# Attention with a delta rule and two feed-forward layers: sixteen weight loads move from SyncE's queue to GpSimd's

## The chip, the core and the metric

The kernel runs on one core of a Trainium2 chip. TensorE (PE) multiplies matrices, VectorE (DVE), ScalarE (ACT) and GpSimd (POOL) compute elementwise, SyncE (SP) computes nothing and issues transfers; the transfers themselves run on 16 DMA engines. The metric is the device time of one execution in microseconds (us), as a median over runs.

## The reference, cut to what matters

```python
# q, k, v: (4, 8, 768, 48), beta: (4, 8, 768)
state = zeros((B, H, D, D))
for t in range(S):
    y[:, :, t] = einsum('bhd,bhde->bhe', q[:, :, t], state)
    v_old = einsum('bhde,bhd->bhe', state, kt)            # kt: normalized k
    state = state + bt * einsum('bhd,bhe->bhde', kt, vt - v_old)
x = y reshaped to (3072, 384)
h = x @ w_in;  g = softplus(h);  x = g @ w_out            # 384 -> 2048 -> 384
h = x @ w_in2; g = h * cos(h);   out = g @ w_out2         # 384 -> 2048 -> 384
```

## The kernel before

The sequence of 768 tokens is cut into 24 chunks of 32. For each group of four chunks the keys and queries are normalized, split into an fp16 high and low part and transposed (`norms`, `prep_k`, `prep_q`), multiplied with each other on TensorE (`gram`, line 606), and a small triangular system is solved on VectorE (`solve`). `step(n)` then carries the state over chunk n and leaves its result y16. A transposing DMA (line 786) writes y16 into `xt`, the input of the first feed-forward layer. Two chunks make a block of 256 tokens: `moe_block(0, j)` multiplies it with the first layer's weights (line 811 into the hidden layer, line 873 out of it). The second layer runs in blocks of 512 tokens after that.

The weights come from HBM as 64-bit floats, sixteen pieces f0 to f15 for each layer, 768 KB each. `conv` loads one piece and turns it into an fp16 high and low part: VectorE at lines 455, 457 and 459 assembles fp32 words in `cv`, ScalarE or VectorE at lines 470 or 474 writes the high part, VectorE at line 480 the low part. A piece lands in the buffer `raw` or in a weight buffer that is not needed yet (order lists print them as w_83, w_84, w_85 and w_86). So a load has to wait until line 459 of the piece before it in that buffer has read it. The transfers between the other stages go through small strips of 32 partitions (`bd_load`: bdKQ, bdA, bdT), four for each.

Nothing of the order is written by hand. `Plan.add` records each operation with its dependencies and the engines it may run on, and `Plan.greedy` simulates the engines and the DMA engines with built-in costs and so fixes, once, in which order each engine gets its instructions; many elementwise operations may go to two engines, and this choice is the planner's as well. On the chip each engine, and SP's and POOL's queue, runs its list strictly in that order: an instruction that waits holds up all behind it.

Of the kernel before, what the change touches and what calls it, by code (L numbers as in the profile page):

```python
# [56 lines left out]
class Plan:  # L57
# [59 lines left out]
    @staticmethod  # L117
    def after(o):

        return 0.65 + 0.9 + o["dma"] + o["slack"] if o["var"][0][0] == "SP" else 0.0  # L120

    def tails(self, succ):
        ops = self.ops
# [9 lines left out]
    def greedy(self, tail, succ, pred, back=None):  # L133
        ops = self.ops
        n = len(ops)
        engs = ("PE", "DVE", "ACT", "POOL", "SP", "-")
        free = {e: 0.0 for e in engs}
        soon = {e: [] for e in engs}
        now = {e: [] for e in engs}
        left = [len(p) for p in pred]  # L140
        ready = [[] for _ in range(n)]
        done = [False] * n
        dma_free = 0.0
        busy = {}
        var = [dict(o["var"]) if back is None else {back[i]: dict(o["var"])[back[i]]} for i, o in enumerate(ops)]

        def release(i):
            for e in var[i]:
                t = 0.0
                for f, end, raw in ready[i]:  # L150
                    t = max(t, end + (self.lat(f, e, raw) if back is None else self.lat(e, f, raw)))
                if back is not None:
                    t += self.after(ops[i])
                heapq.heappush(soon[e], (t, i))

        for i in range(n):
            if not left[i]:
                release(i)
        log = []
        port = {"DVE": 0.0, "POOL": 0.0}  # L160

        def held(e, i, st):

            if back is not None or e not in port or e == "DVE" and not ops[i]["port"]:
                return 0.0
            return max(0.0, port["POOL" if e == "DVE" else "DVE"] - st)

        while len(log) < n:
            best = None
            for e in engs:  # L170
                while soon[e] and (done[soon[e][0][1]] or soon[e][0][0] <= free[e]):
                    t, i = heapq.heappop(soon[e])
                    if not done[i]:
                        heapq.heappush(now[e], (-tail[i], i, t))
                while now[e] and done[now[e][0][1]]:
                    heapq.heappop(now[e])
                if now[e]:
                    st = free[e]
                elif soon[e]:
                    st = soon[e][0][0]  # L180
                else:
                    continue
                if best is None or st < best[0]:
                    best = (st, e)
            st, e = best
            free[e] = st
            while soon[e] and soon[e][0][0] <= st:
                t, i = heapq.heappop(soon[e])
                if not done[i]:
                    heapq.heappush(now[e], (-tail[i], i, t))  # L190
            item = heapq.heappop(now[e])
            i = item[1]
            c = var[i][e] + held(e, i, st)
            urgent = [a for a, b in soon[e] if a < st + c - self.SL and tail[b] > tail[i] + self.MARG and not done[b]]
            if urgent:
                room = min(urgent) - st + self.SL
                fit = [x for x in now[e] if not done[x[1]] and var[x[1]][e] <= room]
                heapq.heappush(now[e], item)
                if not fit:
                    free[e] = min(urgent)  # L200
                    continue
                item = min(fit)
                now[e].remove(item)
                heapq.heapify(now[e])
            i, t = item[1:]
            o, c = ops[i], var[i][e] + held(e, i, st)
            if len(var[i]) > 1:
                pn = self.PEN if st > self.EARLY else self.PEN0
                later = [max(free[e2], t) for e2, c2 in o["var"]
                         if e2 != e and max(free[e2], t) + c2 + pn[e2] < st + c + pn[e]]  # L210
                if later:
                    heapq.heappush(soon[e], (max(st, min(later)) + 1e-3, i))
                    continue
            if e == "SP" and back is None and dma_free > st + c + 0.65 + self.BACKLOG:
                heapq.heappush(soon[e], (dma_free - c - 0.65 - self.BACKLOG + 1e-3, i))
                continue
            done[i] = True
            if e == "PE" and back is None:
                c = self.pe_time(busy, st, c, o["cold"])
            end = st + c  # L220
            free[e] = end + o["hold"]
            if e == "POOL" or e == "DVE" and o["port"]:
                port[e] = end
            if e == "SP" and back is None:
                dma_free = max(end + 0.65, dma_free) + o["dma"]
                end = dma_free + 0.9 + o["slack"]
            log.append((st, end, e, i))
            for s, raw in succ[i]:
                ready[s].append((e, end, raw))
                left[s] -= 1  # L230
                if not left[s]:
                    release(s)
        return log
# [35 lines left out]
def dve(n, fast=False):  # L269
    return 0.068 + n / (1920.0 if fast else 960.0)  # L270
# [6 lines left out]
def pool(n):  # L277
    return 0.149 + n * 0.001883
# [7 lines left out]
def delta_moe_moe_kernel(ctx, tc, q, k, v, beta, mask, w1, w2, out):  # L286
    nc = tc.nc
    eng = {"PE": nc.tensor, "DVE": nc.vector, "ACT": nc.scalar, "POOL": nc.gpsimd, "SP": nc.sync}
# [38 lines left out]
    st = att.tile([P, 2, H, D], F32, name="st")  # L327
# [47 lines left out]
    def put(var, w, r, fn, **kw):  # L375
        return pl.add(var, w, r, fn, **kw)

    def dma(dst, src, w, r, eng_us, issue=0.56, **kw):
        put([("SP", issue)], w, r, lambda e: nc.sync.dma_start(out=dst, in_=src), dma=eng_us, **kw)  # L379

    def copy(out, in_, scale, w, r, n, ps=False, fast=True, only=None, **kw):
        var = [("ACT", act(n, ps)), ("DVE", dve(n, fast and not ps))]
# [38 lines left out]
    def wview(ph, f):  # L421
        return wbuf[ph][f // 2][:, f % 2].bitcast(F16).rearrange("p (o l n) -> p o l n", o=2, l=2)
# [17 lines left out]
    cvn = [0]  # L440

    def conv(ph, f, t, key):
        put([("SP", 0.475)], key, [("wp2",)] if ph else [],
            lambda e: nc.sync.dma_start(out=t(), in_=(w1, w2)[ph][f]), dma=2.18)
        c = cvn[0] % NCV
        cvn[0] += 1
        cv = cvb[c]
        cf = cv.bitcast(F32)
        n = 2 * DM
        ck = [("cv", c, 0), ("cv", c, 1)]  # L450

        def half(b):
            return t().bitcast(I32).rearrange("p o (n two) -> p o n two", two=2)[:, :, :, b]

        put([("DVE", dve(n, True))], ck, key, lambda e: nc.vector.tensor_scalar(
            cv, half(1), 0x07FFFFFF, 3, op0=ALU.bitwise_and, op1=ALU.logical_shift_left), port=True)
        put([("DVE", dve(n))], ck, key, lambda e: nc.vector.scalar_tensor_tensor(
            cv, in0=half(1), scalar=-0x40000000, in1=cv, op0=ALU.bitwise_and, op1=ALU.bitwise_or), port=True)
        put([("DVE", dve(n))], ck, key, lambda e: nc.vector.scalar_tensor_tensor(  # L459
            cv, in0=half(0), scalar=29, in1=cv, op0=ALU.logical_shift_right, op1=ALU.bitwise_or), port=True)  # L460
        if ph:
            copy(cf, cf, W_SC, ck, [], n)
        wk = [("w", ph, f, 0), ("w", ph, f, 1)]

        sc = 1.0 if ph else W_SC
        wv = lambda l: wview(ph, f)[:, :, l]

        def hi(e):
            if e == "ACT":
                nc.scalar.activation(out=wv(0), in_=cf, func=AF.Copy, scale=sc)  # L470
            elif ph:
                nc.vector.tensor_copy(out=wv(0), in_=cf)
            else:
                nc.vector.tensor_scalar_mul(wv(0), cf, sc)

        def lo(e):
            if ph:
                eng[e].tensor_tensor(out=wv(1), in0=cf, in1=wv(0), op=ALU.subtract)
            else:
                nc.vector.scalar_tensor_tensor(wv(1), in0=cf, scalar=sc, in1=wv(0), op0=ALU.mult, op1=ALU.subtract)  # L480

        put([("ACT", act(n)), ("DVE", dve(n, True))], wk, ck, hi, port=True)
        put([("POOL", pool(n)), ("DVE", dve(n))][0 if ph else 1:], wk, ck, lo, port=True)
# [92 lines left out]
    slack = [0.0]  # L576
# [363 lines left out]
    for n in range(4):  # L940
        prep_k(n)
        if n % 2:
            dst, keys = (bdKQ[:, :, 0:12], bdA22)[n // 2], [first[n - 1][1], first[n][1]]
            src = kg0[n // 2][:, :, 16 * C:].rearrange("p n (x t) -> p n x t", t=X2)
# [99 lines left out]
```

## Time and profile before

| | |
|---|---|
| median of 3 runs (lowest to highest) | 1028.8 us (1028.32 to 1029.23) |
| the profiled execution: its own time / its span | 1029.89 us / 1028.1 us |
| PE, DVE, ACT, POOL busy, share of the span | 91%, 65%, 65%, 34% |

The span runs from the first to the last instruction of the profiled execution; 1.8 us of its time lie around it. The page and the views below count in us from the span's start. SPq stands for SP's queue: the time in which it issues a transfer, waits included.

### The profile page before, as it was taken

How to read it: one execution, taken by the hardware profiler on the slowest of the kernel's cores; microseconds unless marked ns; L12 is line 12 of the kernel's file. 1: busy time of each engine (PE TensorE's matmuls, PEld its weight loads, DVE VectorE, ACT ScalarE, POOL GpSimd, SP SyncE). 2: the span in 40 equal slices, each digit the busy share in tenths (PEclk: the TensorE clock that was granted, in tenths of full speed). 3: DMA queues.
4: the chain of work that ended last, by engine and by line, in shares of the span. 5: the costliest groups of instructions: out<-in, count | busy, mean ns of one | idle time of the engine just before them, and what ended most of it. 6: DMA issues, size and time to landing. Idle time of an engine off the chain costs nothing.

```text
span 1028.1 us, 27541 instructions
## 1 busy us (share of the span) xinstructions
PE 933.6 (91%) x11552; PEld 681.6 (66%) x11552; DVE 669.6 (65%) x1199; ACT 665.2 (65%) x1256; POOL 353.4 (34%) x326
## 2 busy tenths in 40 slices
PE   2134899999999999999999999999999999999998
PEld 2124788889998899989998898644444444444443
DVE  9999887468648756964766665685555555455553
ACT  5344669677867877785767788866555555455554
POOL 3022236224523632362233344563332323323222
PEclk9555899999999999999999999999999999999999
DMA  7998796885776678476677842111001010100000
GB/s 202 275 253 213 165 242 155 184 193 129 178 180 134 142 175 181 103 149 162 134 178 204 207 101 78 47 62 62 1 9 54 1 61 1 31 32 1 31 1 32
DMA packets 317020, 121.85 MB, mean 119 GB/s; under 512 B 281440, under 2 KB 296928, under 8 KB 316896
## 3 DMA queue, kind: packets, MB, share of 16 engines
q1 hardware_dynamic: 316896, 120.09, 48.0%
q8 instruction: 91, 1.49, 0.6%
q14 instruction: 33, 0.27, 0.1%
HBM read 73.39 MB, written 37.22 MB: 108 GB/s over the span
## 4 chain that ended last, share of the span: by engine, by line
PE 69%; DVE 10%; ACT 6%; DMA 5%; SPq 5%; issue 3%; POOL 1%; ACTq 0%; DVEq 0%; POOLq 0%
PE psH L811 19%; PE accA L873 14%; PE accB L873 10%; PE psC L811 7%; PE psA L873 6%; PE psC L694 6%; SPq L379 5%; PE psY L811 4%; PE psY L694 2%; PE psA L606 2%; DMA qt<-q_dram 1%; DMA bdA<-kpd 1%; DVE st L404 1%; DVE cv L459 1%; ACT e L828 1%
## 5 line engine op out<-in xcount | busy, mean ns | idle before, releaser
L400 POOL TENSOR_TENSOR g<-g,g 128x512 f16<-128x512 f32 x191 | 228.2, 1195 | 495.3 <-ACT g L388 492.2
L811 PE MATMUL psH<-xt,w 128*128 128x256 f16 x1728 | 225.4, 273 | 1.5 <-DVE w L480 1.1
L388 ACT ACTIVATE g<-g 128x512 f16<-128x512 f32 x192 | 120.5, 628 | 106.5 <-DVE g L404 69.6
L873 PEld LDWEIGHTS <-w 128*128 128x128 f16 x1728 | 160.4, 97 | 18.5 <-issue 0.3
L811 PEld LDWEIGHTS <-w 128*128 128x128 f16 x1728 | 158.7, 98 | 19.8 <-DVE w L480 1.4
L873 PE MATMUL accA<-g,w 128*128 128x256 f16 x1152 | 154.7, 272 | 0.1
L873 PEld LDWEIGHTS <-v 128*128 128x128 f16 x864 | 84.6, 98 | 102.4 <-issue 0.5
L811 PEld LDWEIGHTS <-v 128*128 128x128 f16 x864 | 84.5, 98 | 100.4
L409 ACT ACTIVATE e<-e 128x512 f32<-128x512 f32 x96 | 60.4, 629 | 81.7 <-DVE e L404 81.6
L400 DVE TENSOR_TENSOR g<-psH,e 128x512 f32<-128x512 f32 x96 | 66.0, 688 | 59.8 <-ACT e L411 53.0
L873 PE MATMUL accB<-g,w 128*128 128x256 f16 x576 | 93.1, 272 | 0.0
L694 PEld LDWEIGHTS <-bdA 128*128 128x128 f16 x2256 | 74.1, 98 | 19.0 <-issue 16.7
L811 PE MATMUL psH<-xu,v 128*128 128x512 f16 x351 | 83.4, 379 | 0.0
L811 PE MATMUL psC<-xu,v 128*128 128x512 f16 x342 | 82.1, 379 | 0.0
L873 PE MATMUL accA<-g,v 128*128 128x512 f16 x288 | 78.0, 379 | 0.3 <-POOL g L400 0.3
L873 PE MATMUL accB<-g,v 128*128 128x512 f16 x288 | 77.8, 379 | 0.0
L873 PE MATMUL psA<-g,v 128*128 128x512 f16 x288 | 77.7, 379 | 0.0
L828 ACT ACTIVATE e<-psH 128x512 f32<-128x512 f32 x96 | 56.4, 588 | 28.2 <-PE psH L811 27.8
L694 PEld LDWEIGHTS <-bdKQ 128*128 128x128 f16 x1840 | 61.2, 98 | 16.6 <-issue 15.0
L694 PE MATMUL psC<-u,bdA 128*128 128x48 f16 x1680 | 58.9, 185 | 14.6 <-DMA bdA<-kpd 7.5
L411 ACT ACTIVATE e<-e,hpi 128x512 f32<-128x512 f32 x96 | 69.1, 721 | 2.9
L411 ACT ACTIVATE e<-e 128x512 f32<-128x512 f32 x96 | 59.9, 624 | 1.1
(145 smaller groups left out, 1438.0 us busy)
## 6 DMA issues: line engine op xcount, KB each, us to landing
kpd<-kp SPq DMA_DIRECT2D x24, 512.0 KB, 4.1
bdA<-kpd SPq DMA_DIRECT2D x96, 128.0 KB, 4.5
bdKQ<-kqd SPq DMA_DIRECT2D x92, 128.0 KB, 4.1
kqd<-kq SPq DMA_DIRECT2D x20, 512.0 KB, 5.5
raw<-w_dram SPq DMA_DIRECT2D x12, 768.0 KB, 5.6
w<-w_dram SPq DMA_DIRECT2D x10, 768.0 KB, 6.7
v<-w_dram SPq DMA_DIRECT2D x10, 768.0 KB, 6.1
qt<-q_dram SPq DMA_DIRECT2D x24, 256.0 KB, 4.2
```

Source lines behind the costliest of these rows:

```text
L379: put([("SP", issue)], w, r, lambda e: nc.sync.dma_start(out=dst, in_=src), dma=eng_us, **kw)
L388: nc.scalar.activation(out=out, in_=in_, func=AF.Copy, scale=scale)
L400: put(var, w, r, lambda e: eng[e].tensor_tensor(out=out, in0=a, in1=b, op=op), port=True, **kw)
L404: lambda e: nc.vector.scalar_tensor_tensor(out, in0=a, scalar=s, in1=b, op0=op0, op1=op1), port=True, **kw)
L409: nc.scalar.activation(out=out, in_=in_, func=func, scale=scale)
L411: nc.scalar.activation(out=out, in_=in_, func=func, scale=scale, bias=bias)
L459: put([("DVE", dve(n))], ck, key, lambda e: nc.vector.scalar_tensor_tensor(cv, in0=half(0), scalar=29, in1=cv, op0=ALU.logical_shift_right ...
L606: nc.tensor.matmul(ps[:, h], lhsT=w, rhs=x, start=(i == 0), stop=(i == len(ops) - 1))
L694: nc.tensor.matmul(ps[:, h, 0:D], lhsT=lhs(h), rhs=mov[:, h], start=(first and i == 0 and h == 0), stop=(last and i == len(passes) - 1 and ...
L811: nc.tensor.matmul(hp[:, i] if ph == 0 else hp, lhsT=w[:, l, kc * P:(kc + 1) * P], rhs=xv[:, m * KC + kc], start=(kc == 0 and idx == 0), s ...
L828: nc.scalar.activation(out=ev, in_=hv, func=AF.Abs, scale=sc)
L873: nc.tensor.matmul(acc[c], lhsT=w[:, l, c * P:(c + 1) * P], rhs=rhs, start=(f == 0 and idx == 0 and (ph == 1 or c != 1)), stop=(f == NF - ...
```

## The change

The sixteen loads of the first layer's weights are put on POOL's queue instead of SP's. The planner's cost for the issue is 1.0 us there (0.475 us on SP), and the three places of the planner that treated a transfer by the name SP now ask whether the operation is a transfer at all. `dma()` gets a parameter for the issuing engine, which no call uses. All other transfers, the second layer's sixteen loads among them, stay on SP.

```diff
-        return 0.65 + 0.9 + o["dma"] + o["slack"] if o["var"][0][0] == "SP" else 0.0
+        return 0.65 + 0.9 + o["dma"] + o["slack"] if o["dma"] else 0.0
...
-            if e == "SP" and back is None and dma_free > st + c + 0.65 + self.BACKLOG:
+            if o["dma"] and back is None and dma_free > st + c + 0.65 + self.BACKLOG:
...
-            if e == "POOL" or e == "DVE" and o["port"]:
+            if e == "POOL" and not o["dma"] or e == "DVE" and o["port"]:
                 port[e] = end
-            if e == "SP" and back is None:
+            if o["dma"] and back is None:
...
-        put([("SP", 0.475)], key, [("wp2",)] if ph else [],
-            lambda e: nc.sync.dma_start(out=t(), in_=(w1, w2)[ph][f]), dma=2.18)
+        put([("SP", 0.475)] if ph else [("POOL", 1.0)], key, [("wp2",)] if ph else [],
+            lambda e: eng[e].dma_start(out=t(), in_=(w1, w2)[ph][f]), dma=2.18)
```

Since the planner plans anew, every engine's list changes. Three places matter here.

POOL at the start of the program, before: it clears buffers and then multiplies keys of the first group (`kt`, `kp`).

```order
L416 MEMSET bdA_102 128x1024
L416 MEMSET bdKQ 128x2048
L416 MEMSET bdA_102 128x1536
L416 MEMSET bdA_102 128x3072
L416 MEMSET bdT 128x1024
L416 MEMSET st 128x768
L400 ISA
L400 TENSOR_TENSOR kt_114<-kt_114,n_119 128x384
L400 TENSOR_TENSOR kp_123<-kt_114,kp_123 128x256
```

POOL at the same place with the change (three small memsets stand where the dots are, and more loads follow the last row):

```order
L416 MEMSET bdA_102 128x1536
L416 MEMSET st 128x768
L444 DMA raw_87<-w_dram 128x768
...
L444 DMA w_83<-w_dram 128x768
L416 MEMSET bdA_102 128x3072
L444 DMA w_84<-w_dram 128x768
L416 MEMSET t_134 128x1024
L416 MEMSET bdT 128x1024
L416 MEMSET bdA_102 128x1024
L444 DMA raw_87<-w_dram 128x768
L444 DMA w_83<-w_dram 128x768
```

Loads f0, f1 and f2 now stand among POOL's memsets, f3 and f4 behind them, and the first group's multiplications of keys have left POOL for DVE. Thirteen of the sixteen loads stand ahead of POOL's first TENSOR_TENSOR; f13, f14 and f15 stand between later ones.

DVE in the conversion of the first pieces, with the change, from the instruction behind the one that frees `raw` (f0) to the first one that reads f3 from it:

```order
L459 SCALAR_TENSOR_TENSOR cv_89<-w_83,cv_89 128x768
L541 STREAM_TRANSPOSE w_86<-ka_126 128x128
L474 TENSOR_SCALAR w_79<-cv_89 128x2x384
L404 SCALAR_TENSOR_TENSOR b_109<-bt,b_109 128x384
L480 SCALAR_TENSOR_TENSOR w_79<-cv_88,w_79 128x2x384
L455 TENSOR_SCALAR cv_88<-w_84 128x768
L404 SCALAR_TENSOR_TENSOR abuf<-psA,mask_sb,abuf 128x8x16
L457 SCALAR_TENSOR_TENSOR cv_88<-w_84,cv_88 128x768
L404 SCALAR_TENSOR_TENSOR abuf<-psH_138,mask_sb,abuf 128x8x16
L459 SCALAR_TENSOR_TENSOR cv_88<-w_84,cv_88 128x768
L480 SCALAR_TENSOR_TENSOR w_79<-cv_89,w_79 128x2x384
L455 TENSOR_SCALAR cv_89<-raw_87 128x768
```

Eleven rows stand ahead of the reading of f3 here. Before, 55 stood there, nearly the whole triangular solve of the first group among them; the conversion of f3 now stands ahead of the solve, and so does the first part of f4's.

SP around the two transposes of the first block's y16 (chunk 0, then chunk 1), before:

```order
L379 DMA bdA_102<-kq_128 32x12x64 x4
L379 DMA bdKQ<-kqd 32x32x64
L444 DMA raw_87<-w_dram 128x768
L379 DMA bdKQ<-kqd 32x32x64 x3
L786 DMA_TRANSPOSE xt_90<-y_111 128x6x128
L444 DMA w_86<-w_dram 128x768
L379 DMA bdT<-tgd 32x8x64 x4
L786 DMA_TRANSPOSE xt_90<-y_111 128x6x128
```

And with the change:

```order
L379 DMA kt_113<-k_dram 128x384
L786 DMA_TRANSPOSE xt_90<-y_111 128x6x128
L379 DMA bdA_102<-kq_128 32x12x64
L379 DMA bdKQ<-kqd 32x32x64
L379 DMA bdA_102<-kq_128 32x12x64 x3
L379 DMA bdKQ<-kqd 32x32x64 x3
L786 DMA_TRANSPOSE xt_90<-y_111 128x6x128
```

The transpose of chunk 0 now stands ahead of the eight strips that it stood behind, and no weight load stands between the two transposes.

## Rows read from the trace of the kernel before

**Rows 1.** The page: span, and busy time of each engine.
```profile
span 1028.1 us, 27541 instructions
PE 933.6 (91%) x11552; PEld 681.6 (66%) x11552; DVE 669.6 (65%) x1199; ACT 665.2 (65%) x1256; POOL 353.4 (34%) x326
```

**Rows 2.** Windows up to and after the first feed-forward matmul: length, busy time by engine.
```profile
0.00:108.60 108.60, 34.68 (x873) 32.50 (x874) 100.65 (x200) 46.67 (x98) 23.17 (x24) 0.63 0.86 234
108.60:220.00 111.40, 103.44 (x1829) 93.05 (x1827) 78.87 (x159) 81.05 (x170) 38.38 (x40) 0.99 0.81 188
```

**Rows 3.** PE's timeline at the first matmul of line 811: start, length.
```profile
108.46 5.23 PE L811 MATMUL psH<-xt,w 128*128 128x256 f16 x36
```

**Rows 4.** DVE's waits, 0 to 125 us: total, times, longest.
```profile
DVE abuf L404 <- ACT abuf L388: 1.7, 1, 1.7
DVE cv L455 <- DMA raw<-w_dram: 1.5, 1, 1.5
DVE y L404 <- ACT y L388: 1.4, 1, 1.4
```

**Rows 5.** SP's queue, timeline: weight loads and transposes before the first block.
```profile
81.52 0.86 SPq L444 DMA_DIRECT2D raw<-w_dram  x1
...
98.02 3.04 SPq L786 DMA_TRANSPOSE xt<-y  x1
101.17 0.51 SPq L444 DMA_DIRECT2D w<-w_dram  x1
...
103.95 1.22 SPq L786 DMA_TRANSPOSE xt<-y  x1
```

**Rows 6.** Timeline: DVE frees raw; DVE and ACT write y16 of chunks 0 and 1.
```profile
73.50 1.48 DVE L459 SCALAR_TENSOR_TENSOR cv<-raw,cv 128x768 int32<-128x768 int32 x1
...
89.15 0.54 DVE L404 SCALAR_TENSOR_TENSOR y<-psY,y 128x384 f16<-128x384 f32 x1
...
102.84 0.49 ACT L388 ACTIVATE y<-psY 128x384 f16<-128x384 f32 x1 [2.67 <-DMA xt<-y]
```

**Rows 7.** Groups of DVE by shape, 0 to 130 us: count, busy, mean ns.
```profile
L480 DVE SCALAR_TENSOR_TENSOR w<-cv,w 128x768 f16<-128x768 f32 x14 | 13.4, 970 | 0.0
L459 DVE SCALAR_TENSOR_TENSOR cv<-w,cv 128x768 int32<-128x768 int32 x10 | 10.2, 1026 | 0.0
L457 DVE SCALAR_TENSOR_TENSOR cv<-w,cv 128x768 int32<-128x768 int32 x10 | 9.3, 950 | 0.0
L404 DVE SCALAR_TENSOR_TENSOR b<-bt,b 128x384 f16<-128x384 f32 x6 | 3.3, 550 | 0.0
L455 DVE TENSOR_SCALAR cv<-w 128x768 int32<-128x768 int32 x10 | 5.5, 555 | 0.1
L404 DVE SCALAR_TENSOR_TENSOR abuf<-psA,mask_sb,abuf 128x128 f32<-128x128 f32 x5 | 2.2, 442 | 0.0
L474 DVE TENSOR_SCALAR w<-cv 128x768 f16<-128x768 f32 x3 | 1.7, 553 | 0.0
L541 DVE STREAM_TRANSPOSE w<-ka 128x128 f32<-128x128 f32 x4 | 1.1, 266 | 0.0
```

**Rows 8.** Loads into raw, 0 to 120 us: issue on SP in ns, landing (min/median/max).
```profile
L444 SPq DMA_DIRECT2D raw<-w_dram x6: 376/410/864, 4.0 to 112.6; - x6
DMA to landing us min/median/max: 5.4/6.4/10.5
```

**Rows 9.** DMA issues, 0 to 160 us: two kinds of 32 KB strips, median landing.
```profile
bdT<-tgd SPq DMA_DIRECT2D x12, 32.0 KB, 4.5
raw<-tgd SPq DMA_DIRECT2D x4, 32.0 KB, 2.1
```

**Rows 10.** Timeline: a DVE multiplication alone, and one beside POOL's.
```profile
11.36 0.55 DVE L400 TENSOR_TENSOR kt<-kt,n 128x384 f32<-128x384 f32 x1
...
68.05 1.36 POOL L400 TENSOR_TENSOR kt<-kt,n 128x384 f32<-128x384 f32 x1 [21.38 <-DMA qt<-q_dram]
...
68.65 1.18 DVE L400 TENSOR_TENSOR kt<-kt,n 128x384 f32<-128x384 f32 x1
```

More of the change, by code (lines that the diff above doesn't have):

```diff
@@ L376, in put, with dma @@
         return pl.add(var, w, r, fn, **kw)
-    def dma(dst, src, w, r, eng_us, issue=0.56, **kw):
-        put([("SP", issue)], w, r, lambda e: nc.sync.dma_start(out=dst, in_=src), dma=eng_us, **kw)
+    def dma(dst, src, w, r, eng_us, issue=0.56, on="SP", **kw):
+        put([(on, issue)], w, r, lambda e: eng[e].dma_start(out=dst, in_=src), dma=eng_us, **kw)
     def copy(out, in_, scale, w, r, n, ps=False, fast=True, only=None, **kw):
```

## The prediction

> **What bounds the kernel now.** I read the page first: TensorE is busy for 933.6 of 1028.1 us [rows 1], so 94.5 us of idle are all that a change of order can win. The windows say where they lie. Up to 108.6 us PE is busy for 34.7 us only, which leaves 73.9 us idle; the next 111.4 us have 8.0 us of idle, and 12.6 us are left for the remaining 808 us [rows 2]. The line between the two regimes is the first matmul of line 811, at 108.46 us [rows 3]: from there on TensorE nearly always has a block of the feed-forward layer to work on. So the end of the kernel comes earlier by about as much as that first block starts earlier, and the sixteen loads all lie ahead of it or close behind it. What the program does from 220 us on is no subject of this change, except that the new plan shuffles it.
>
> What bounds the first 108.6 us is not a transfer. DVE is busy for 100.65 of them, ACT for 46.7, POOL for 23.2 [rows 2]. The busy times of DVE are overlapped a little, since successive spans reach about 0.08 us into one another, but the reader should see an engine that hardly ever stops. DVE's list of waits shows where it does stop, and three entries matter: 1.7 us for ACT's `abuf`, 1.5 us for a load of `raw`, 1.4 us for ACT's `y` [rows 4]. The first block waits for y16 of chunk 1, whose second half DVE writes right behind that last wait; its transpose is issued at 103.95 us [rows 5]. So a move of transfers can help only through DVE's waits or DVE's list.
>
> **What the change does to SP.** Sixteen issues of a median 0.41 us [rows 8] leave SP's queue, 6.6 us in all. SP's time isn't on the path by itself; what counts is what stood behind a load. Two of DVE's three waits are of that kind. The `raw` that DVE lacked was free at 73.50 + 1.48 = 74.98 us [rows 6], but SP issued the load at 81.52 us only [rows 5], 6.5 us later, behind strips. On POOL nothing stands ahead of that load but other loads and a memset, and in the new order of DVE 13.7 us of DVE's work lie between the freeing and the next reading of that buffer (summed as for f3 below), against a landing time of 6.4 us [rows 8]. This wait goes: -1.5 us. The wait for `y` came from the first transpose: y16 of chunk 0 was complete at 89.7 us [rows 6], SP issued its transpose at 98.02 us [rows 5], and ACT could not overwrite y16 before it landed and waited 2.67 us [rows 6]. In the new list this transpose stands ahead of the eight strips and the load that held it up. This wait goes too: -1.4 us.
>
> **What it does to DVE.** I summed DVE's lists up to the second half of y16 of chunk 1, each instruction at the mean of its group (the largest are in [rows 7]) less 0.075 us of overlap: 192 instructions and 94.8 us before, 184 and 93.4 us now, so -1.4 us. DVE takes on a 2048-word memset and three copies of bdT, and pushes some work of the second group behind that point. The wait for `abuf` is filled: the conversions of f2 to f4 now stand there, -1.7 us.
>
> **What it does to POOL.** Each load costs POOL its issue. No row shows a transfer issued there. From below the price is SP's 0.41 us [rows 8], from above an elementwise instruction of POOL, 1.36 us [rows 10]; I take 0.9 us, in the middle. Sixteen of these are 14.4 us on an engine that was busy for 23.2 of 108.6 us, and its memsets are needed late, so as work they cost nothing. What they can do is make loads late. Between the freeing of `raw` and the reading of f3 the new list holds eleven DVE instructions; with line 459 at 1.03, 541 at 0.27, 474 at 0.55, 404 at 0.55 and twice 0.44, 480 at 0.97 twice, 455 at 0.56, 457 at 0.95 and 459 at 1.03 [rows 7] that is 7.76 us, less 11 overlaps 6.9 us. The load needs 0.9 + 6.4 = 7.3 us. So DVE waits 0.4 us for f3, and by the same sum 0.6 us for f14 (6.7 us); f4 has 8.1, f13 8.9 and all others over 10 us. Before, the shortest such distance was 8.4 us. Cost: +1.0 us. Behind a load that waits on POOL stand, late in the stage, keys of the second group and a rounding of the state; there the loads' conditions are DVE instructions that precede in time whatever produces these operands, so I set nothing for them. If that cover fails, a wait of up to one landing, 6.4 us, would pass to DVE.
>
> The Trainium skill speaks of this in "SBUF — State Buffer", section "SBUF: two separate sides": a transfer issued by GpSimd has its descriptors written by GpSimd's own cores, and a DVE instruction in a two-port mode locks them out meanwhile. The rows show instructions of line 455 and 474 at 0.55 us where others of the same 768 elements take 0.95 [rows 7], which fits such a mode; one of them lies in f3's distance and none right behind the freeing of f14's buffer, so by that page the sum would be worse by about 0.55 us, an estimate. No trace here shows such a transfer yet.
>
> **Sum.** -1.5 - 1.4 - 1.4 - 1.7 + 1.0 = -5.0 us, against the profiled execution's own 1029.9 us (span 1028.1 and 1.8 around it), so 1024.9 us; against the median of 1028.8 us, which lies 1.1 us lower, 1023.8 us. I forecast **1024 us**.
>
> The bounds: a gain that I left out is that strips no longer queue behind a 768 KB load. bdT's strips, some of them behind such a load, land in 4.5 us and the same size without one in 2.1 us [rows 9], so up to 2.4 us more where DVE isn't the limit: -7.4 us, 1021.4 us. Losses are the rivals.
>
> **Rival 1, only issue time is saved.** DVE remains the bound and the waits turn up again elsewhere, since whatever frees DVE earlier makes it reach the next operand earlier. For it: the three waits are separate events, and DVE ran without a pause for most of the stage, so the chain of PE, ACT and DVE behind it may have little slack. Against it: two of the three come from SP's order alone. Then only the shorter list and the tight loads are left, -1.4 + 1.0 = -0.4 us, **1028.4 us**. In the skill's "DMA: Bandwidth & Descriptors", section "Issuing engines are not separate DMA queues", stands the rule for this: transfers of all issuers share the same 16 engines, and another issuer saves only the time of the issue. The window's share of busy DMA engines, 0.86 [rows 2], agrees that they are well filled.
>
> **Rival 2, GpSimd's loads land late, slower.** The landing of loads into `raw` reaches 10.5 us [rows 8]. With 0.9 + 10.5 us the waits are 4.5 us for f3, 4.7 for f14, 2.5 for f13 (8.9) and 0.7 for f15 (10.7), 12.4 us, and f4 is covered by f3's wait. Against the 6.0 us of gains that is +6.4 us, **1035 us**. It decides from the landing at which f3, f14 and f13 together take 6.0 us: 3 x (0.9 + landing) - 22.5 = 6.0, a landing of 8.6 us. For it: the order was planned with shorter distances than before, and the page's lock would add to each. Against it: at f3 DVE converts while few transfers run, and the median is 6.4 us.
>
> **Rival 3, DVE is slowed.** A DVE multiplication beside a POOL instruction took 1.18 us, alone 0.55 [rows 10], so +0.63 us. If each issue on POOL does that to one DVE instruction, 16 x 0.63 = 10.1 us: -5.0 + 10.1 = +5.1 us, **1034 us**. It decides from 5.0 / 16 = 0.31 us for each load. Against it: that POOL instruction reads two tensors, an issue reads none.
>
> **How the numbers follow.** The forecast has a chance of 0.50, rival 1 0.20, rival 2 0.20, rival 3 0.10. A difference of 0.2%, 2.1 us, is about what a measurement of this kernel can tell from no change. The forecast's cases end below 1026.7 us (0.50 faster), rival 1 within 1026.7 to 1030.9 (0.20 same), rivals 2 and 3 above (0.30 slower). The forecast's own range is 1021 to 1026.7 us. To leave out no more than 0.2 the range goes to 1020 us, a little below the lower bound for the reshuffled order behind 220 us, and to 1034 us, rival 3's price, with the worse half of rival 2 left out.
>
> **What would show it.** In the profile after: the first matmul of line 811 near 108.5 - 5 = 103.5 us; no `raw` wait and no `y` wait of DVE; the first transpose issued within a microsecond or two of chunk 0's y16; waits of DVE at line 455 for f3 and f14 under 1 us; issues on POOL near 0.9 us and landings near 6.4 us; PE's idle time after the first block again near 20 us. The forecast is wrong if line 811 starts early and PE's idle time behind it grows by as much, if DVE's waits at line 455 sum to over 6 us, or if DVE's groups of [rows 7] get longer beside POOL's issues.

## The result, and the profile after

The changed kernel takes 1040.3 us (median of 4 runs, 1038.63 to 1041.14), the kernel before 1029.01 us (4 runs, 1028.32 to 1029.32): a ratio of 1.0103 with a 95% interval of 1.008 to 1.0126. It is 1.0% slower, where 1024 us was forecast, with a range up to 1034 us.

The page (span, busy time of each engine) of the changed kernel, its two windows that answer to [rows 2], and the window up to its own first matmul of line 811:

```profile
span 1038.6 us, 27585 instructions
PE 937.1 (90%) x11552; PEld 683.4 (66%) x11552; DVE 673.4 (65%) x1199; ACT 665.9 (64%) x1257; POOL 356.9 (34%) x341
```
```profile
0.00:108.60 108.60, 29.75 (x768) 27.65 (x768) 98.28 (x191) 42.81 (x91) 23.89 (x36) 0.72 0.81 229
108.60:220.00 111.40, 98.73 (x1696) 88.83 (x1694) 78.84 (x157) 76.53 (x161) 38.86 (x41) 0.92 0.81 171
0.00:113.40 113.40, 31.43 (x808) 29.25 (x809) 102.90 (x197) 44.92 (x97) 25.47 (x39) 0.71 0.82 223
```

PE did 4.9 us less up to 108.6 us (29.75 against 34.68) and 4.7 us less in the window behind (98.73 against 103.44). Together that is 9.6 of the 10.5 us by which the span grew. (The granted clock of the second window was 0.92 against 0.99, so more work is missing there than the busy time says: 1696 matmuls against 1829.) The edge at 108.6 us is the old kernel's, though. Cut at the changed kernel's own first matmul of line 811, PE's idle time ahead of it is 113.40 - 31.43 = 82.0 us, where [rows 2] give 73.9, and from there to 220 us it is 9.6 us against 8.0. So most of the loss stands ahead of the first block, and a smaller part behind it.

DVE's waits up to 220 us, the two longest that are new (total, times, longest):

```profile
DVE kq L541 <- DMA kqd<-kq: 6.9, 1, 6.9
DVE w L480 <- ACT w L470: 5.9, 1, 5.9
```

The forecast's own signs are there: the `raw` and `y` waits of [rows 4] are gone, nothing waits at line 455 in this trace, and chunk 0's transpose goes out at 95.91 us, right behind its y16. PE's idle time behind the start of the first block, forecast near 20 us again, is 1038.6 - 937.1 - 82.0 = 19.5 us. But the first matmul of line 811 comes 4.95 us later than in [rows 3], not 5 us earlier.

**The first loss.** SP's and POOL's queues (start, length), ACT, DVE and PE of the changed kernel near 30 us:

```profile
22.27 6.97 SPq L379 DMA_DIRECT2D bdA<-w  x8
...
23.75 0.53 POOL L444 DMA_DIRECT2D raw<-w_dram  x1 [13.13 <-DVE cv L459]
24.61 0.53 POOL L444 DMA_DIRECT2D w<-w_dram  x1 [0.34 <-DVE w L541]
...
33.97 1.23 PE L606 MATMUL psH<-w,bdA 128*128 128x32 f16 x40 [8.42 <-issue]
...
35.24 0.51 ACT L388 ACTIVATE abuf<-psH,mask_sb 128x128 f32<-128x128 f32 x1 [7.55 <-PE psH L606]
35.76 0.84 ACT L470 ACTIVATE w<-cv 128x768 f16<-128x768 f32 x1
...
36.63 0.96 DVE L480 SCALAR_TENSOR_TENSOR w<-cv,w 128x768 f16<-128x768 f32 x1 [5.85 <-ACT w L470]
...
113.41 3.45 PE L811 MATMUL psH<-xt,w 128*128 128x256 f16 x18
```

Eight small strips of `bdA` leave SP from 22.27 us on. In the middle of them POOL issues f3 (`raw`) and f4 (`w`). PE then stands for 8.42 us before the Gram matmuls that read the strips (the row names no releaser; that it is the strips follows from their landing, shown next), ACT waits for PE, line 470 stands behind that wait in ACT's order, and DVE behind line 470. The list of DMA issues gives the strips' landing, first for the kernel before (17 to 25 us), then for the changed one (21 to 30 us):

```profile
bdA<-w SPq DMA_DIRECT2D x8, 48.0 KB, 2.5
```
```profile
raw<-w_dram POOLq DMA_DIRECT2D x1, 768.0 KB, 6.4
bdA<-w SPq DMA_DIRECT2D x8, 48.0 KB, 7.5
```

And this is the order that SP's queue of the kernel before had kept:

```profile
18.29 6.00 SPq L379 DMA_DIRECT2D bdA<-w  x8
...
26.05 0.38 SPq L444 DMA_DIRECT2D raw<-w_dram  x1
26.52 0.38 SPq L444 DMA_DIRECT2D w<-w_dram  x1
```

There f3 and f4 stood behind the strips.

**The second loss.** DVE and SP of the changed kernel near 180 us:

```profile
176.67 0.70 DVE L539 STREAM_TRANSPOSE kq<-kp 128x512 f32<-128x512 f32 x1
...
179.60 0.57 SPq L379 DMA_DIRECT2D kqd<-kq  x1
...
184.23 0.31 DVE L541 STREAM_TRANSPOSE kq<-ka 128x128 f32<-128x128 f32 x1 [6.85 <-DMA kqd<-kq]
```

For chunk 8 the new plan enters the store `kqd<-kq` between the two transposes that write the chunk's keys. The transpose of line 541 then has to wait until the store has landed, and step 4 waits behind it on DVE. In the kernel before the store comes behind both transposes, and no instruction of line 541 waits for a store there. While DVE waits (177.0 to 184.3 us), PE is busy for 3.30 of the 7.30 us, and its granted clock, 1.00 there, is 0.68 in the mean of the 10.7 us behind. By the index ranges in the code the store reads no word that line 541 writes; that the program makes it wait all the same, because it compares whole ranges, is argued from the code only.

### The profile page after: what moved, and what is told of

Read it like the earlier page. It is cut to its first block, busy times and chain, and to the rows that moved or that the text cites. A ratio compares the mean times of both kernels' runs of the same rounds, so it can differ in the third digit from the quotient of the medians.

```text
span 1038.6 us, 27585 instructions
## 1 busy us (share of the span) xinstructions
PE 937.1 (90%) x11552; PEld 683.4 (66%) x11552; DVE 673.4 (65%) x1199; ACT 665.9 (64%) x1257; POOL 356.9 (34%) x341
## 4 chain that ended last, share of the span: by engine, by line
PE 60%; DVE 13%; ACT 9%; SPq 5%; issue 5%; DMA 5%; POOL 2%; DVEq 0%; ACTq 0%; POOLq 0%
PE psH L811 16%; PE accA L873 12%; PE accB L873 9%; PE psC L811 7%; PE psA L873 6%; SPq L379 5%; PE psC L694 4%; PE psY L811 4%; PE psY L694 2%; DMA bdA<-kpd 2%; DVE g L400 1%; ACT kp L388 1%; ACT e L828 1%; DVE tmpd L400 1%; POOL g L400 1%
## 5 line engine op out<-in xcount | busy, mean ns | idle before, releaser
L694 PEld LDWEIGHTS <-bdKQ 128*128 128x128 f16 x1840 | 60.4, 98 | 12.5 <-issue 10.5
```

The costliest lines, as they stand in the source:

```text
L694: nc.tensor.matmul(ps[:, h, 0:D], lhsT=lhs(h), rhs=mov[:, h], start=(first and i == 0 and h == 0), stop=(last and i == len(passes) - 1 and ...
```

## The experiments

Theory A: bytes of the loads that POOL issues move while SP's strips do, and slow them. Theory B: the new plan's order costs the time, whoever issues. Theory C: POOL's issues slow DVE. Theory D, added after the first four runs: the store's wait is the second half of the loss.

How fine these can be read: the kernel before alone spread from 1020.5 to 1034.0 us in the runs below, so ratios have intervals of some 0.25%. A trace tells more up to the end of block 1 (DVE's last `xs` of that block): two traces of the changed kernel agree there to 0.7 us (222.72 and 222.02) and differ by 4.7 us in span (1038.6 and 1033.9); two of the kernel before differ there by 2.3 us (211.87 and 209.56). Runs g2 and g3 below are the same program up to chunk 0's y and differ there by 3.2 us. Differences of up to 3 us are taken as nothing. A table of all runs stands behind the experiments.

**Plan and issuer apart.** Run e1 is the kernel before with one line changed, e2 the changed kernel with the issuer put back:

```diff
-            lambda e: nc.sync.dma_start(out=t(), in_=(w1, w2)[ph][f]), dma=2.18)
+            lambda e: (nc.sync if ph else nc.gpsimd).dma_start(out=t(), in_=(w1, w2)[ph][f]), dma=2.18)   # e1
-            lambda e: eng[e].dma_start(out=t(), in_=(w1, w2)[ph][f]), dma=2.18)
+            lambda e: nc.sync.dma_start(out=t(), in_=(w1, w2)[ph][f]), dma=2.18)                         # e2
```

> The plan of the kernel before (same order of PE, DVE and ACT to the instruction), but the sixteen loads are issued by GpSimd at their planned places. Theory A (a load on a queue of its own is no longer held behind the small strips that SP's queue had ahead of it, and takes the DMA engines from them): slower than the kernel before by 3 to 8 us, 1032 to 1037 us, with bdA's or bdKQ's strips landing in more than 4 us in place of 2.5. Theory B (the new plan's order costs the time, not the queue): within 2 us of the kernel before, 1027 to 1031 us. Theory C (GpSimd's issues slow DVE): slower by 2 to 10 us with the same instructions of DVE longer and strips as before.

> The new plan (same order of PE, DVE and ACT as the changed kernel), but the sixteen loads are issued by SyncE again, at the places in the plan where GpSimd issued them. Theory A: the strips of bdA land in about 2.5 us again, DVE's wait of 5.9 us at 31 us is gone or under 2 us, and the time is 1025 to 1034 us. Theory B: the order itself costs, 1038 to 1041 us, with the wait of 5.9 us still there. Theory C: as A, but strips as slow as in the changed kernel and DVE's instructions shorter.

e1: ratio 1.0084 (1.0059 to 1.0109), first line 811 at 113.10 us. SP, POOL and ACT of e1:

```profile
19.56 6.13 SPq L379 DMA_DIRECT2D bdA<-w  x8
...
23.76 0.60 POOL L444 DMA_DIRECT2D raw<-w_dram  x1 [8.39 <-DVE cv L459]
...
34.57 0.48 ACT L388 ACTIVATE abuf<-accA,mask_sb 128x128 f32<-128x128 f32 x1 [6.37 <-PE accA L606]
```
And DVE's longest wait up to 125 us:
```profile
DVE abuf L404 <- ACT abuf L388: 6.5, 1, 6.5
```

With the old order on PE, DVE and ACT, the issuer alone brings the first loss: only the last two strips come after f3, so their median is 3.2 us (over 4 was expected), but the last one decides, and DVE's wait for `abuf` is 6.5 us where [rows 4] has 1.7. DVE's instructions are not longer (line 480 takes 971 ns, 970 in [rows 7]), so theory C falls. e2: ratio 1.0051 (1.0024 to 1.0077), line 811 at 110.50 us. The strips took 5.9 us, not 2.5 as A expected, and SP's timeline says why:

```profile
22.09 2.57 SPq L379 DMA_DIRECT2D bdA<-w  x4
24.77 0.55 SPq L444 DMA_DIRECT2D raw<-w_dram  x1
25.42 1.58 SPq L444 DMA_DIRECT2D w<-w_dram  x1
27.11 1.43 SPq L379 DMA_DIRECT2D bdA<-w  x2
```

The new plan, which priced f3 and f4 on another queue, put them ahead of the last four strips (and f5 ahead of the last two); on SP they then stand before them. The time, 1032.76 us, lies in A's range all the same. And DVE's wait at line 541 is there in e2 as well, 8.1 us. So neither A nor B is the whole.

**The bytes.** e3 cuts f3 and f4 to 48 KB each, e4 all loads from f3 on but f6 and f7, so that most of these weights is left out of the result; each engine's order stays. (The expectations say 24 KB. The edit takes 48 of 768 words of 64 bits in each partition, and the trace lists 48.0 KB.)

```diff
-            lambda e: eng[e].dma_start(out=t(), in_=(w1, w2)[ph][f]), dma=2.18)
+            lambda e, z=DM if ph or f not in (3, 4) else 48: eng[e].dma_start(
+                out=t()[:, 0:1 + z // DM, 0:z], in_=(w1, w2)[ph][f][:, 0:1 + z // DM, 0:z]), dma=2.18)
```

> The changed kernel with the loads of f3 and f4 cut to 48 of 1536 words of a partition (24 KB for each 768 KB; most of these two blocks of weights is left out); the order is that of the changed kernel. Theory A: the strips of bdA land in about 2.5 us, PE's first Gram matmul comes some 4 us earlier than at 33.97 us, DVE's 5.9 us wait falls below 2 us; the first matmul of line 811 comes 3 to 5 us earlier than at 113.41 us and the time is 1034 to 1037 us. Theories B and C: 1039 to 1041 us, with the wait of 5.9 us where it was.

> As the run before, but eleven of the sixteen loads are cut to 24 KB (f3 to f5 and f8 to f15; most of these blocks of weights is left out). Theory A: the strips of step 2 before the first matmul of line 811 are quick as well, that matmul comes at 104 to 109 us, and the time is 1027 to 1034 us. Theories B and C, in which the issues and the order matter and not the bytes: 1038 to 1041 us.

e3: strips of `bdA` in 3.1 us, DVE's 5.9 us wait down to 0.5, line 811 at 107.88 us, ratio 1.0039 (1.002 to 1.0059). That is a little more than A expected: 5.5 us earlier at line 811, where 3 to 5 were expected, and 1031.64 us, 2 us below the range. e4, PE's timeline:

```profile
104.55 3.10 PE L811 MATMUL psH<-xt,w 128*128 128x256 f16 x18
```

The bytes of the loads are the first loss: without most of them the first block starts 8.9 us earlier than in the changed kernel, and 1.4 to 3.9 us earlier than in the kernel before, close to the 103.5 us forecast. Still e4 is slower than the kernel before (1.0033, 1.0009 to 1.0058). Part of the lead goes where DVE waits 7.8 us at line 541, from 167.6 to 175.4 us; f7 shows below what the rest is.

**The store.** A function gets the finished list; `behind(i, j)` puts operation i right behind j. In f5 that changes no engine's order, only which of two instructions waits for the other; f7 adds the cut of e4, f8 real loads kept out of the strips' way:

```diff
+    behind(find(("kqd", 8))[0], find(("kq", 0, 3))[1])            # f5, f7, f8, f9
+    behind(load[3], strips[-1], "SP")                             # f8, f9
+    behind(load[4], load[3], "SP")                                # f8, f9
+    for i in (load[3] + 1, load[3] + 2, load[4] + 1, load[3] + 3, load[3] + 4, load[8], load[4] + 2):
+        behind(i, k)      # k: the last abuf instruction of the first group, then the one just placed
+        k = i
```

> The changed kernel once more, unedited, on the chip that runs the next three, so that these can be compared with it. All theories: 9 to 13 us slower than the kernel before.

> The changed kernel; each engine's instructions stay in the same order, only the store of chunk 8's keys and queries (kqd<-kq) is entered in the program behind the transpose of that chunk's tail keys (line 541), so that the transpose no longer waits for the store to land. Theory D (the second half of the loss is this one wait, which the new order makes): DVE's wait of 6.9 us at 177 to 184 us falls below 1 us, y of chunk 4 comes at 183 to 185 us in place of 190.2, and the time falls by 5 to 7 us against the changed kernel. Rival (the store is only the last to finish, and DVE would wait there for ACT's ka or POOL's kp anyway): the wait stays over 4 us and the time falls by less than 2 us.

> The kernel of the run before with eleven of the sixteen loads cut to 24 KB as well (f3 to f5 and f8 to f15; most of these blocks of weights is left out). If theory A (bytes of GpSimd's loads in the way of strips) and theory D are the whole loss: first matmul of line 811 at 104 to 105 us, y of chunk 4 at 173 to 176 us, 3 to 6 us below the kernel before, which is the prediction's -5 us. If a third cause is at work behind 110 us: the lead at line 811 is given back again and the time is within 2 us of the kernel before.

> The changed kernel with the store entered behind the transpose, and with the loads of f3 and f4 issued by SyncE right behind the eight strips of bdA, their conversions on DVE moved to just before the solve of the first group (nothing left out). Theories A and D: strips of bdA land in 2 to 3.5 us, the first matmul of line 811 comes at 107 to 109 us, y of chunk 4 at 176 to 179 us, and the time is 1 to 5 us below the kernel before. Rival (DVE waits for f3 in place of the strips): a wait of 3 us or more at line 455 near 35 us, line 811 at 111 us or later, and the time 2 us or more above the kernel before.

c0: 1.009 (1.0068 to 1.0112), so the change is as slow on this chip. f5's DVE at the same place:

```profile
178.20 0.71 DVE L539 STREAM_TRANSPOSE kq<-kp 128x512 f32<-128x512 f32 x1
179.99 0.31 DVE L541 STREAM_TRANSPOSE kq<-ka 128x128 f32<-128x128 f32 x1 [1.09 <-ACT ka L388]
```

The wait for the store is gone, 1.09 us for ACT stay. Block 1 ends at 217.96 us in place of 222.02, and chunk 4's y at 186.5 in place of 190.0. The time falls by 2.3 us only (1033.34 against 1035.61, ratio to the kernel before 1.0066, 1.0042 to 1.0089), and that interval overlaps c0's, so this pair alone does not show a gain in time. D is right on the wait, and 5 to 7 us was too much for it: DVE's wait for ACT's y at 202 us grows from 0.7 to 3.5 us. With the loads cut as well the gain is clear: e4 has 1.0033 (1.0009 to 1.0058), f7 0.999. f7: line 811 at 104.54 us, chunk 4's y at 176.9, ratio 0.999 (0.9975 to 1.0005). With both causes away nothing of the 1% is left, but the 3 to 6 us of gain are not there either; by f7's expectation this is the sign of a third cause. PE's idle time says what it is. Up to the first matmul of line 811 PE is idle for 104.54 - 31.48 = 73.1 us in f7, for 108.46 - 34.54 = 73.9 us in the kernel before and 105.91 - 34.53 = 71.4 us in its second trace, b0. The new order puts 64 matmuls of step 2 behind that first matmul (808 stand ahead of it instead of 872), so it comes earlier without PE being idle for less. The lead is work put off.

f8: strips in 2.1 us, line 811 at 108.84, 1.0023 (1.0000 to 1.0046), nothing left out. The strips and line 811 came as expected; the time, expected 1 to 5 us below the kernel before, did not.

**Fewer loads on POOL.** g2 is e1 with f3 and f4 left on SP; g3 is g2 with chunk 0's transpose ahead of six of its eight strips; f9 is f8 with f13's load on SP behind chunk 1's transpose. b0 is the kernel before, traced on the same chip; its line 811 comes at 105.91 us, where 108 to 109 was expected.

```diff
+            lambda e: (nc.gpsimd if not ph and f not in (3, 4) else nc.sync).dma_start(...)               # g2, g3
+    behind(xt[0], log[nxt - 1][3])       # g3, h1: transpose of chunk 0, once its y16 is written
+    behind(load[13], xt[1], "SP")        # f9
+    behind(load[12], load[11])           # h1
```

> The kernel before, unedited, on the chip of the next three runs, for a trace of it there. All theories: the time of the kernel before, the first matmul of line 811 at 108 to 109 us.

> The kernel before with fourteen of the sixteen loads issued by GpSimd, f3 and f4 left with SyncE behind the strips of bdA (same order of PE, DVE and ACT as the kernel before). Theory A: DVE's wait for abuf, 6.5 us when GpSimd issued f3 and f4 too, is 2.5 us or less again, the first matmul of line 811 comes at 106.5 to 109 us in place of 113.1 us, and the time is within 3 us of the kernel before. Theory C or another (GpSimd's issues as such, or the other loads): the first matmul of line 811 stays at 111 us or later, and the time is 4 us or more above the kernel before.

> The kernel of the run before with the transpose of chunk 0's y moved, on SyncE, ahead of six of the eight strips that stood before it. The prediction's step on the y wait (-1.4 us): DVE's waits for y fall below 0.5 us and the first matmul of line 811 comes 1 to 2 us earlier than in the run before. Rival (the strips then land later and the wait turns up there): no earlier than in the run before.

> The kernel with the store behind the transpose and f3 and f4 on SyncE, with f13's load moved to SyncE as well, right behind the transpose of chunk 1's y, and its first conversion on DVE moved four instructions later. Theory A (f13's bytes delay step 2's strips of bdKQ, which stand before line 811 on PE): PE's wait for these strips, 3.9 us at 107 us, falls below 2 us, the first matmul of line 811 comes at 104.5 to 106.5 us in place of 108.8 us, and the time falls by 1 to 3 us against that kernel. Rival (the transposes and strips are slow by themselves, or DVE now waits for f13): line 811 at 108 us or later.

g2 did not come out as theory A said. Strips of `bdA<-w` are back at 2.4 us and the `abuf` wait is down to 1.1 us, but line 811 comes at 116.02 us (1.0065, 1.0038 to 1.0091). SP, PE and DVE of g2:

```profile
43.94 12.55 SPq L379 DMA_DIRECT2D bdA<-kpd  x4
...
62.53 1.12 PE L694 MATMUL psC<-u,bdA 128*128 128x48 f16 x24 [9.73 <-DMA bdA<-kpd]
...
63.69 0.56 DVE L404 SCALAR_TENSOR_TENSOR bt<-psC,bt 128x384 f32<-128x384 f32 x1 [6.65 <-PE psC L694]
```

The collision moved to the next strips: POOL issues three more loads at 43.45, 47.56 and 53.21 us, and four strips of `bdA<-kpd` take 12.55 us on SP and land in 10.2 us. By the timing it is the same cause at another place, though no run cuts these bytes alone; protecting one set of strips doesn't protect the next. How hard they collide differs: in g3, the same program up to there, the four take 7.83 us on SP and land in 8.7 us, in e1 5.55 and 6.3, in the kernel before 5.36 and 6.2. g3 stands at 111.42 us and 1.0046 (1.0025 to 1.0066), 4.6 us before g2; but chunk 0's y was 3.2 us earlier already, ahead of the moved transpose, so it decides nothing. f9: PE's wait of 3.9 us for step 2's strips is gone, line 811 at 107.17 us (104.5 to 106.5 expected), 1.0017 (0.9998 to 1.0036), which is not measurably below f8 (1 to 3 us expected). f8 and f9 are the best of the complete versions with loads on POOL and no faster than the kernel before.

**The two waits by themselves.** h1 keeps all loads on SP and only moves f12's load ahead of four strips, and the transpose as in g3.

> The kernel before with all loads still on SyncE and only two of its transfers moved there: the load of f12 ahead of four strips of bdA, the transpose of chunk 0's y ahead of six strips. The prediction's steps on the raw wait (-1.5 us) and the y wait (-1.4 us), without GpSimd: both waits gone, the first matmul of line 811 at 105 to 107 us, the time 1 to 3 us below the kernel before. Rival 1 of the prediction (the waits turn up elsewhere): the time within 1 us of the kernel before, with a new wait of DVE or PE of 1 us or more for strips that now stand behind these two.

The longest of DVE's waits up to 125 us, first h1, then b0:

```profile
DVE bt L404 <- PE psC L694: 4.2, 2, 2.2
```
```profile
DVE g L400 <- ACT e L411: 1.2, 1, 1.2
DVE y L404 <- ACT y L388: 1.1, 1, 1.1
```

Neither wait is left in h1, and it is no faster: 1.0015 (0.9995 to 1.0035), line 811 at 108.06 us (105 to 107 expected). Two waits for PE, 4.2 us together, have come up, and PE waits just ahead of them for strips (5.43 us for `bdA<-kq`, 4.76 us for `bdKQ<-kqd`), as rival 1 has it. And in b0, the second trace of the kernel before, the `raw` wait doesn't occur at all.

**Strips and loads by themselves.** m1 and m2 issue six strips three times in each setting:

```python
if s == "B": load(nc.gpsimd, 0, f)                                # beside; F: two of them
if s == "C": load(nc.sync, 0, f)                                  # ahead in the same queue; G: two
if s == "E": load(nc.scalar, 0, f)                                # beside, ScalarE's queue; H: two
strips(s)                                                         # six on SyncE; A: alone
if s == "D": load(nc.sync, 0, f)                                  # behind
```

> Not the kernel but its disputed transfers by themselves (nothing of the reference is computed; the output is zeros): six strips of 48 KB from SBUF to SBUF on SyncE, three times each in seven settings: A alone; B beside one 768 KB load that GpSimd issues at the same time; C behind that load in SyncE's queue; D ahead of it there; E beside it on ScalarE's queue; F beside two loads of GpSimd; G behind two in SyncE's queue. Theory A, any second queue: strips land in 2 to 2.5 us in A and D, 4 us or more in B and E, 6 us or more in F and G. Theory A, only GpSimd's queue gets ahead: E as A. If a load does not disturb strips at all: all near 2 to 2.5 us, and theory A falls. At the end four small DVE instructions alone and four beside three POOL memsets of 1024 words: 0.1 to 0.3 us alone; over 0.9 us for the first one beside them if the memsets lock DVE out.

> The transfers by themselves once more (nothing of the reference is computed), with each setting started only when the loads of the one before have landed, which in the first try disturbed setting E; H is new: beside two loads on ScalarE's queue. If any second queue gets in the way: E as B, near 4.4 us, and H as F, near 6.2 us. If only GpSimd's queue does: E and H near 2 us. The three POOL memsets now run beside the last four small DVE instructions: over 0.9 us for the first of these if a memset locks DVE out, 0.18 us as alone if not.

m1 gave 2.0 (A), 4.4 (B), 3.8 (C), 2.0 (D), 6.2 (F) and 5.3 us (G); its E (2.7) was disturbed by D's load. The DMA issues of m2, last column the median landing:

```profile
stripA<-src SPq DMA_DIRECT2D x18, 48.0 KB, 2.0
stripB<-src SPq DMA_DIRECT2D x18, 48.0 KB, 4.4
stripC<-src SPq DMA_DIRECT2D x18, 48.0 KB, 3.6
stripD<-src SPq DMA_DIRECT2D x18, 48.0 KB, 2.0
stripE<-src SPq DMA_DIRECT2D x18, 48.0 KB, 4.2
stripF<-src SPq DMA_DIRECT2D x18, 48.0 KB, 6.2
stripG<-src SPq DMA_DIRECT2D x18, 48.0 KB, 5.3
stripH<-src SPq DMA_DIRECT2D x18, 48.0 KB, 5.7
```

A load beside the strips doubles their landing, on POOL's queue as on ACT's. One ahead of them in their own queue costs nearly as much. Only a load behind them costs nothing. The Trainium skill says in "DMA: Bandwidth & Descriptors", section "Issuing engines are not separate DMA queues", that transfers of all issuers run on the same 16 engines and interleave: B and E agree. It adds that another issuer saves only the time of the issue. These rows show one thing more: it also gives up an order (D 2.0, B 4.4).

All runs (us; line 811 and block 1 from the traces):

| run | first line 811 | end of block 1 | ratio to before (other intervals in the text) |
|---|---|---|---|
| before, b0 | 108.46, 105.91 | 211.87, 209.56 | b0: 0.998 (0.9958 to 1.0002) |
| after, c0 | 113.41, 114.19 | 222.72, 222.02 | 1.0103 (1.008 to 1.0126), 1.009 |
| e1, old plan on POOL | 113.10 | 217.26 | 1.0084 |
| e2, new plan on SP | 110.50 | 219.41 | 1.0051 |
| e3 / e4, loads cut | 107.88 / 104.55 | 216.84 / 213.60 | 1.0039 / 1.0033 |
| f5, store | 114.64 | 217.96 | 1.0066 |
| f7, store and loads cut | 104.54 | 208.43 | 0.999 |
| f8 / f9 | 108.84 / 107.17 | 211.27 / 212.33 | 1.0023 / 1.0017 |
| g2 / g3 | 116.02 / 111.42 | 221.68 / 218.82 | 1.0065 / 1.0046 |
| h1 | 108.06 | 214.20 | 1.0015 |

At the end of block 1 the two causes add up: the bytes cost 222.02 - 213.60 = 8.4 us with the store's wait and 217.96 - 208.43 = 9.5 without it, the wait 4.1 and 5.2 us. Both away, block 1 ends 1.1 to 3.4 us before the two traces of the kernel before, which is hardly more than the noise. The number of matmuls done by 220 us says the same: 2700 and 2748 in the kernel before and b0, 2461 and 2468 in the changed kernel and c0, 2561 in f5, 2654 in e4, 2748 in f7.

## Why the prediction was wrong, step by step

**The step that failed first** is the term for the strips. The sum has none, and the bounds name it as a gain: "a gain that I left out is that strips no longer queue behind a 768 KB load", up to 2.4 us from [rows 9]. It has the wrong sign. I read there that a load ahead of a strip delays it, which is right (C and G), and took the queue for an obstacle only. It was also what kept f3 and f4 behind the strips of `bdA` (D), and on a queue of their own they run beside them (B and F): 8 to 9 us at the end of block 1. The sentence that "on POOL nothing stands ahead of that load" was true, and that was the trouble.

**The second failed step** is that the end "comes earlier by about as much as that first block starts earlier". e4 starts 1.4 to 3.9 us earlier than the kernel before and ends later; f7 starts as early and ends at the same time. Two things were left out. The new order was counted up to chunk 1 and called a shuffle behind 220 us; the store's wait, 4 to 5 us at the end of block 1, lies between these two. And the start of the first block was taken for PE's idle time ahead of it, which is no shorter (73.1 us in f7, 73.9 and 71.4 before), since 64 matmuls were put off.

**The two waits**, -1.5 and -1.4 us: they went, as said, but h1 shows that their going is worth nothing measurable, and b0 that one of them is not there in every execution. DVE's list and the `abuf` wait (-1.4 and -1.7) can be read with the bytes out of the way only: chunk 1's y is then at 99.98 us (e4) against 103.92 and 101.46 before, 1.5 to 3.9 us earlier, and in the time of f7 none of it is left (0.999, 0.9975 to 1.0005). DVE does not have less to do either: it runs 1199 instructions in both kernels, busy for 669.6 us before and 673.4 after; the eight that are missing up to that y come later.

**Tight loads**, +1.0: in the first trace of the changed kernel DVE waits for no load, in c0 for 0.44 us for f3, as the sum has it, and for 1.46 us for a load near 112 us. The term was right in kind and not the loss. An issue on POOL is 0.53 us at the median, not 0.9, and landings are 5.8 us (`raw`) and 7.8 us (`w`). So rival 2 is out; that its 1035 us lies nearest is chance. Rival 3, DVE slowed by each issue, is out too (e1). Rival 1 was right on the gains (h1); that its -0.4 us is near f7 (1024.86 against 1025.67) tests little, since f7 leaves most of the weights out. No rival had the losses. Of the instructions at 0.55 us two lie in f3's distance (lines 474 and 455), not one as the prediction says; no run shows them slowing POOL's issues, which took 0.53 to 0.72 us.

**"Its memsets are needed late, so as work they cost nothing."** As work; but three of them now run beside DVE's line 509, and that one instruction takes 1.87 us where it took 0.31. What it costs the kernel can't be seen: in e2 it takes 0.18 us and the first Gram matmul is no earlier (20.95 us, 21.18 in the changed kernel). Both are some 3.4 us behind the kernel before (17.61 us), so that delay belongs to the new order.

Open: how much of the 1% in time belongs to the store and how much to the bytes. The store is worth 0.24% by c0 and f5 and 0.43% by e4 and f7, and with intervals of some 0.25% on each ratio these do not differ. And no complete version with loads on POOL was found that is faster than the kernel before.

## What to carry to other kernels

A queue is also an order. Before a large transfer leaves it, list the small ones that stood ahead of it and are waited for; they now share the DMA engines with it, and on which engine's queue it went matters little. When a planner makes the new order, compare not only the stage that the change is about, but every store and reader of a shared tile whose places were swapped. And judge an earlier start of a stage by the idle time of the engine that limits it, not by the start of one instruction: other work may only have been put off.

## What the runs showed that was not expected

A 48 KB strip lands in 2.0 us alone, in 4.2 to 4.4 beside one 768 KB load and in 5.7 to 6.2 beside two, with little difference between the two issuers. SP's time to issue strips can grow too (12.55 us for four in g2, 5.36 us for the same four in the kernel before), but did not in e1 (5.55 us). And a POOL memset holds up a small DVE instruction, which m2 shows by itself: the four instructions of 32 elements on line 85 ran beside two memsets of 0.95 and 0.98 us (ns min/median/max):

```profile
L85 DVE TENSOR_SCALAR small<-small x4: 181/500/889, 237.5 to 239.5; 128x32 f32<-128x32 f32 x4
```

Alone each takes 0.18 us. Beside the memsets the first two took 0.82 and 0.89 us, a little under the 0.9 us expected, and the last two 0.18. The Trainium skill, "SBUF — State Buffer", section "SBUF: two separate sides", has DVE in a two-port mode and POOL lock each other out of a shared port for a whole instruction; 0.889 us, nearly the length of a memset, agrees; that this DVE instruction runs in such a mode no row shows.
